# A fused attention and MLP kernel on one core: w_in's first columns sliced by contraction rows, tokens 512 to 767 as two units, later output stores, whole visits

## The chip, the core and the metric

One core of a Trainium2 chip. The time is that of one execution of the program on the device, in microseconds (us); lower is better. The core has a matmul engine (TensorE, PE in the profile; PEld is its loading of weights), a vector engine (VectorE, DVE), a scalar engine (ScalarE, ACT), a general engine (GpSimd, POOL) and an engine that here only issues transfers (SyncE, SP). Each runs its own instruction list in order, and waits for others by semaphores. 16 DMA engines move data between the chip's memory (HBM) and on-chip memory; transfers are issued here by SP and POOL. Matmuls write to PSUM, eight banks of 2 KB in each of 128 partitions.

## The reference

Linear attention with decay, and then a two-layer network, over 4 batches, 8 heads, 768 positions, 64 numbers a head:

```python
for b in range(nb):                      # blocks of 64 positions
    intra = einsum('bhic,bhjc->bhij', qb, kb) * Dmask      # lam ** (i-j), j <= i
    intra = einsum('bhij,bhjd->bhid', intra, vb)
    inter = einsum('bhid,bhde->bhie', qb * lam_pow, kv_state)
    out[:, :, sl] = intra + inter
    kv_state = lam_block * kv_state + einsum('bhsd,bhse->bhde', kb * rev_pow, vb)
...
x = out.transpose(0, 2, 1, 3).reshape(3072, 512)
h = x @ w_in                                               # 512 -> 2048
g = where(h >= 1, h, where(h <= -1, 0, (h + 1) ** 2 / 4))
return g @ w_out                                           # 2048 -> 512
```

All inputs and the output are float32.

## The kernel before

**Attention.** q and k are multiplied by powers of lam that depend on the position alone, so that the decay needs no mask of its own, and are rounded to bf16 in the same step ("cast"). What is left is causal linear attention: scores of a block, a mask, scores times v, and the state (a running sum of k times v) times q.

- The first 512 tokens run as four *units* of 256 tokens and 4 heads (`NU = 4`; functions `e_...`, keys `("...", "e", u)`). A unit loads with two neighbouring tokens to a partition, 512 bytes in a row (`e_load`, L313). PE transposes q and k (`e_t`, L334), ACT or DVE copies the result (`e_tc`, L348), PE computes scores (`e_s`, L381), DVE masks them (`e_m`, L393), PE adds to the state (`e_upd`, L356) and forms state times q (`e_sp`, L399) and scores times v (`e_o`, L414; from unit 2 on a PE drain stands ahead of it), and ACT copies the result to `xT` (`e_x`, L431). In a unit the tokens stand even ones first, so the output tiles of these tokens are stored by halves, every other row (`f_out`, L681).
- Tokens 512 to 767 are chunks 4 and 5, of 128 tokens and all 8 heads, with a code of their own: casts at L465, transposes on PE (`f_t`, L471), scores (`f_s`, L565), output and state (`f_visit` and `f_o`, L583 to L602).
- Chunks 6 to 23 (batches 1 to 3) are cast by POOL (q, k; L468) and ACT (v; L458), transposed by a DMA from on-chip memory to on-chip memory that SP issues (`f_tx`, L483), and then computed by 64x64 matmuls in *visits* (`f_visit2`, L536): scores times v and the second half of state times q of chunk c, and, with them, `f_ahead(c + 1)` (L529): the first half of state times q, the scores, and k times v of chunk c + 2 (L515). For `SPLIT = (9, 11)` the visit leaves `f_ahead` out, which then stands as an operation of its own (`("s", 10)`, `("s", 12)`).

Chunks are loaded with 256 bytes in a row (`f_load`, L438), six buffers deep for each of q, k and v.

**Layers 1 and 2.** Six supertiles of 512 tokens. Layer 1 (`f_l1`, L615) multiplies a slice of w_in with `xT`; a group of 8 matmuls of 256 columns (16 of 128 in supertile 1) fills a PSUM bank of the pool `pp_h` (2 banks) or, for three early groups, of `pp_y` (2 banks). ACT applies a Relu (`f_r`, L629), DVE does the rest of the activation in three steps (`f_g`, L631). Layer 2 (`f_l2`, L650) adds up 16 matmuls in `pp_y`, ACT copies them out (`f_y`, L677) into one of eight output buffers (`OB = 8`), POOL stores them (the last supertile: SP).

**Weights.** Nine slices, loaded by POOL with a conversion to bf16 (`load_w`, L171). The first two are 256 columns of w_in each, all 512 rows of them; the rest have 512 columns, or 512 rows of w_out. Loads of chunk 4 wait for weight slice 7 (`GL`, L732).

**What sets the order.** `add(key, engine, ns, fn, needs, due, ...)` describes every operation with a cost in ns, what it needs and a due time; `run_plan` (L196) works through them as if time passed: on the engine that is free first it takes, of the operations whose needs are met by then, the one due first, and writes the instructions down in that order. On the chip each engine then keeps to this list. Layer 1 and 2 are due one `STEP` apart along `l_seq` (L711), which both kernels share; an attention visit is due 3 us before the layer-1 group that needs it, but is placed as soon as it is ready and nothing is due before. Stores of the first four tiles wait for the visit of chunk 9 + y (L896), later ones only for their tile and the plan's delay.

Of the kernel before, what the change touches and what calls it, by code (L numbers as in the profile page):

```python
# [8 lines left out]
F32 = mybir.dt.float32  # L9
# [14 lines left out]
def kernel(  # L24
# [30 lines left out]
    NU = 4  # L55
# [4 lines left out]
    XT, MG, NQT, NQK, NVS, NUB, RING = 6, 6, 4, 4, 5, 4, 3.5  # L60
# [36 lines left out]
    NE = 4  # L97
    pos_ei = const.tile([128, 2, 2], I32)
    nc.gpsimd.iota(pos_ei, pattern=[[2 * C, 2], [1, 2]], base=-S // 2, channel_multiplier=2)
# [68 lines left out]
    WSL = [(0, 0, 2), (0, 2, 4), (0, 4, 8), (0, 8, 12), (0, 12, 16),  # L168
           (1, 0, 4), (1, 4, 8), (1, 8, 12), (1, 12, 16)]

    def load_w(i):  # L171
        x, lo, hi = WSL[i]
        if x == 0:
            return nc.gpsimd.dma_start(out=w_in_sb[:, :, lo * 128:hi * 128], in_=w_in_r[:, :, lo * 128:hi * 128])
        return nc.gpsimd.dma_start(out=w_out_sb[:, lo:hi, :], in_=w_out_r[:, lo:hi, :])

    def w_of(x, f):
        return [("w", i) for i, (y, lo, hi) in enumerate(WSL) if y == x and lo <= f < hi][0]

# [16 lines left out]
    def run_plan(free):  # L196
# [14 lines left out]
        for x in reversed(topo):  # L211
            d = [u.due - u.ns - x.extra - LAT for u in users[x.key] if not u.dma]
            x.due = min(d + ([x.own] if x.own is not None else []), default=1e9)
            if x.dma or x.key[0] in ("l1", "l2"):
                x.due = x.own
# [92 lines left out]
    def get_ub(c):  # L308
        if c not in ubt:
            ubt[c] = ubp.tile([128, HP, D], BF16, name="ub", tag="ub")  # L310
        return ubt[c]

    def e_load(u, x):  # L313
# [3 lines left out]
        ld_dma["e", u, x] = nc.sync.dma_start(  # L317
            out=t, in_=(q, k, v)[x][0, HR * r:HR * r + HR, s0:s0 + 2 * C, :].rearrange("h (p j) d -> p h (j d)", j=2))
        qkv_ld["e", u, x] = t

    def e_cast(u, x, eng):
        sc, r = divmod(u, 2)
        nm, dct = (("qs", qs), ("ks", ks), ("vs", vs))[x]
        t = qkp.tile([128, 2, HR, D], BF16, name=nm, tag=nm)
# [22 lines left out]

    def e_tc(u, i, eng):  # L348
# [7 lines left out]
    def e_upd(u, a):  # L356
        r, after = u % 2, a == 0 and u > 0
# [13 lines left out]
    def e_st(u, a, eng):  # L371

        if u >= NU:
            dst = get_ub(NU - 1)[:, 2 * (u % 2):2 * (u % 2) + 2, :]
        else:
            t = ubt["e", u, a] = ubp.tile([128, 2, D], BF16, name="ue", tag="ue", bufs=4)
            dst = t
# [21 lines left out]
    def e_sp(u):  # L399
        sc = u // 2  # L400
        po = pot["e", u] = [pp_y.tile([128, MS], F32, name="py", tag="py")[:, 0:256].rearrange("p (h q) -> p h q", h=2)
                            for _ in range(2)]
# [9 lines left out]
        e_upd(u, 1)  # L412

    def e_o(u):  # L414
        sc, po, after = u // 2, pot["e", u], u < NU - 2
# [15 lines left out]
    def e_x(u, a, eng):  # L431
        sc, r = divmod(u, 2)
        off = 2 * C * sc + C * a
        (nc.scalar.copy if eng is nc.scalar else eng.tensor_copy)(
            get_xT(0)[:, 2 * r:2 * r + 2, off:off + C], pot["e", u][a])


    def f_load(c, x, wait):  # L438
# [3 lines left out]
        if wait is not None:  # L442
            tc.add_manual_dep(d.ins, w_dma[wait].ins.name, SYNC)
# [8 lines left out]
    def pair(t, hp):  # L452
        return t[:, 2 * hp:2 * hp + 2, :].rearrange("p a d -> p (a d)")

    def cast(c, x, eng):
        if x == 2:
            t = vs[c] = qkp.tile([128, H, D], BF16, name="vs", tag="vs")
# [6 lines left out]
        if c < NCB:  # L464
            eng.tensor_tensor(t, qkv_ld[c, x], tb, op=AX.mult)  # L465
        else:
            h4 = "p (g i) d -> p g i d"
            eng.tensor_tensor(t.rearrange("p (i g) d -> p g i d", g=2), qkv_ld[c, x].rearrange(h4, g=2),  # L468
                              tb.rearrange(h4, g=2), op=AX.mult)

    def f_t(c):  # L471
        ptt[c] = (pp_o.tile([128, 2, HP, 128], BF16, name="po", tag="po") if c == NU
                  else pp_s.tile([128, 2, HP, 128], BF16, name="ps", tag="ps"))
        for i, x in ((1, ks), (0, qs)):
            for hp in range(HP):
                nc.tensor.transpose(out=ptt[c][:, i, hp, :], in_=pair(x[c], hp), identity=ident)

    def f_tc(c, i):
        dct, nm = ((qT, "qT"), (kT, "kT"))[i]
        t = dct[c] = qtp.tile([128, HP, 128], BF16, name=nm, tag=nm)  # L480
        nc.vector.tensor_copy(t, ptt[c][:, i])
# [83 lines left out]
    def f_s(c):  # L565
        for par in range(2):
            pst[c, par] = pp_s.tile([128, HP, 128], F32, name="ps", tag="ps")
        for hp in range(HP):
            for par in range(2):
                for a in range(2):  # L570
                    nc.tensor.matmul(pst[c, par][HD[a], hp, :], lhsT=kT[c][HD[par], hp, HD[a]],  # L571
                                     rhs=qT[c][HD[par], hp, :], start=True, stop=True, skip_group_check=True)

    def f_m(c, par):
        if par == 0:
            sc_sb[c] = scp.tile([128, 2, HP, 128 if c < NCB else 64], BF16, name="sc" if c < NCB else "sd", tag="sc" if c < NCB else "sd")
        if c < NCB:
            nc.vector.tensor_tensor(sc_sb[c][:, par], pst[c, par], _bc(causal, 1, HP), op=AX.mult)
        else:
            nc.vector.tensor_tensor(sc_sb[c][:, par], pst[c, par], _bc(diag, 1, HP), op=AX.mult)  # L580

    def f_o(c):
# [347 lines left out]
```

## Time and profile before

| | us |
|---|---|
| three runs | 208.47, 209.11, 209.81 |
| their median | 209.11 |
| the profiled execution | 207.5 |
| its span (first to last instruction) | 205.8 |
| first layer-1 matmul starts | 16.2 |
| last layer-2 matmul starts | 202.7 |
| TensorE busy | 196.9 |
| ACT, DVE, POOL busy | 120.4, 140.8, 72.3 |
| share of the 16 DMA engines' time, SP's queue and POOL's | 70.5%, 20.6% |

The clock granted to TensorE is 1.00 in every stretch. The profile lists each instruction with its line, its engine, the tile that it writes, start and length, and, where its engine stood idle before it, what ended that idle time ("<-"). Its chain of waits is the work that ended last, followed back step by step; "issue" in it is time in which nothing that the profile shows was waited for. A DMA's landing is given as the time from its issue.

### The profile page before, as it was taken

The page shows a single profiled execution, that of the slowest core. Times are in us where ns is not written, and L with a number is a line of the kernel's source. Part 1 is how long each engine was busy: PE and PEld are TensorE (multiplying, and loading weights), DVE is VectorE, ACT ScalarE, POOL GpSimd, SP SyncE. Part 2 cuts the span into 40 slices and gives each one's busy share as a digit, 9 for nine tenths or more (in the row PEclk, how much of TensorE's full clock was granted, in tenths as well). Part 3 has the DMA queues.
Part 4 walks back from the last instruction along what each step waited for, and adds up shares of the span by engine and source line. Part 5 has one row for each costly group of instructions (what it writes and reads, how often), then busy time and mean ns, then how long its engine had stood idle before and what let it go on. Part 6 is the DMA issues. An engine that isn't in the chain of part 4 may idle for free.

```text
span 205.8 us, 6360 instructions
## 1 busy us (share of the span) xinstructions
PE 196.9 (96%) x2721; PEld 135.7 (66%) x2753; DVE 140.8 (68%) x251; ACT 120.4 (59%) x225; POOL 72.3 (35%) x95
## 2 busy tenths in 40 slices
PE   7789999999999999999999999999999999999994
PEld 2558875457867867767757777766766766666643
DVE  4694997254885985859985998978876656364510
ACT  4476763327676756675674877486585465463421
POOL 6898000264225363474365255445331011010000
PEclk9999999999999999999999999999999999999999
DMA  5999999999999999999999999999942011011112
GB/s 163 301 235 196 198 206 212 219 220 183 132 183 247 138 201 208 258 195 243 193 183 292 173 218 253 194 180 275 204 109 74 3 43 62 0 51 54 51 51 102
DMA packets 94909, 34.48 MB, mean 168 GB/s; under 512 B 82210, under 2 KB 93218, under 8 KB 94882
## 3 DMA queue, kind: packets, MB, share of 16 engines
q1 hardware_dynamic: 88464, 24.65, 70.5%
q0 software_dynamic: 6416, 9.44, 20.6%
q8 instruction: 21, 0.34, 0.7%
q14 instruction: 6, 0.05, 0.1%
q10 hardware_dynamic: 2, 0.00, 0.0%
HBM read 27.26 MB, written 6.29 MB: 163 GB/s over the span
## 4 chain that ended last, share of the span: by engine, by line
PE 91%; SPq 3%; DMA 3%; issue 2%; DVE 0%; ACT 0%
PE ph L621 41%; PE py L654 38%; SPq L317 3%; DMA x1f<-in_k_dram 3%; PE py L664 2%; PE ps L515 1%; PE py L621 1%; PE ps L507 1%; PE pu L542 1%; PE po L542 1%; PE po L526 1%; PE py L423 1%; PE pu L526 0%; DVE ks L330 0%; PE ps L571 0%
## 5 line engine op out<-in xcount | busy, mean ns | idle before, releaser
L621 PE MATMUL ph<-xT,w_in_sb 128*128 128x256 bf16 (+1 forms) x872 | 94.0, 257 | 0.0
L629 ACT ACTIVATE r<-ph,one 128x512 bf16<-128x512 f32 x93 | 63.8, 687 | 45.2 <-PE ph L621 38.7
L621 PEld LDWEIGHTS <-w_in_sb 128*128 128x128 bf16 x896 | 76.3, 98 | 19.6 <-issue 0.2
L654 PE MATMUL py<-w_out_sb,gT 128*128 128x512 bf16 x338 | 86.0, 379 | 2.3 <-issue 1.1
L654 PEld LDWEIGHTS <-gT 128*128 128x128 bf16 x368 | 34.9, 98 | 28.4
L637 DVE TENSOR_SCALAR t<-r 128x1024 bf16<-128x1024 bf16 x48 | 22.5, 468 | 32.8 <-ACT r L629 32.4
L645 DVE TENSOR_TENSOR gT<-w,t 128x1024 bf16<-128x1024 bf16 x48 | 39.0, 812 | 1.4
L640 DVE TENSOR_TENSOR w<-r,t 128x1024 bf16<-128x1024 bf16 x48 | 38.8, 808 | 1.6
L468 POOL TENSOR_TENSOR kq<-x1f,tkd 128x512 bf16<-128x512 f32 x18 | 20.4, 1131 | 33.2 <-DMA x1f<-in_k_dram 23.4
L468 POOL TENSOR_TENSOR kq<-x0f,tqd 128x512 bf16<-128x512 f32 x18 | 19.7, 1093 | 23.8 <-DMA x0f<-in_q_dram 23.7
L688 POOL DMA_DIRECT2D out_dram<-osb x16 | 9.2, 573 | 32.6 <-ACT osb L679 32.6
L679 ACT COPY osb<-py 128x512 f32<-128x512 f32 x23 | 13.5, 585 | 11.3 <-PE py L654 6.9
L580 DVE TENSOR_TENSOR sd<-ps,diag 128x256 bf16<-128x256 f32 x36 | 13.5, 417 | 3.7 <-PE ps L515 3.5
L458 ACT CAST vs<-x2f 128x512 bf16<-128x512 f32 x20 | 12.4, 618 | 4.9 <-DMA x2f<-in_v_dram 4.5
L554 DVE TENSOR_TENSOR st<-st,ps 128x256 f32<-128x256 f32 x30 | 12.5, 415 | 0.5
L559 ACT CAST us<-st 128x512 bf16<-128x512 f32 (+1 forms) x18 | 10.4, 579 | 1.3 <-DVE st L554 1.2
L465 POOL TENSOR_TENSOR kq<-x0f,tqd 128x512 bf16<-128x512 f32 x2 | 2.4, 1178 | 20.8 <-DMA x0f<-in_q_dram 20.8
L563 ACT CAST xT<-po 128x256 bf16<-128x256 f32 x18 | 6.8, 377 | 4.5 <-PE pu L526 4.0
L563 ACT CAST xT<-pu 128x256 bf16<-128x256 f32 x18 | 6.7, 374 | 2.3 <-PE po L526 2.3
L542 PEld LDWEIGHTS <-vs 64*64 64x64 bf16 x288 | 3.7, 107 | 6.5 <-issue 5.9
L396 DVE TENSOR_TENSOR sc<-ps,mask 128x512 bf16<-128x512 f32 x8 | 5.2, 682 | 2.1 <-PE ps L388 2.1
L515 PE MATMUL ps<-vs,kq 64*64 64x64 bf16 x264 | 6.2, 196 | 0.0
(96 smaller groups left out, 134.3 us busy)
## 6 DMA issues: line engine op xcount, KB each, us to landing
x0f<-in_q_dram SPq DMA_DIRECT2D x24, 256.0 KB, 5.6
x1f<-in_k_dram SPq DMA_DIRECT2D x24, 256.0 KB, 4.8
x2f<-in_v_dram SPq DMA_DIRECT2D x24, 256.0 KB, 5.4
out_dram<-osb POOLq DMA_DIRECT2D x16, 256.0 KB, 4.0
w_out_sb<-in_moe_w_out_dram POOLq DMA_DIRECT2D x4, 512.0 KB, 14.4
w_in_sb<-in_moe_w_in_dram POOLq DMA_DIRECT2D x3, 512.0 KB, 7.8
out_dram<-osb POOLq DMA_DIRECT2D x8, 128.0 KB, 4.6
out_dram<-osb SPq DMA_DIRECT2D x3, 256.0 KB, 2.0
```

The costliest lines, as they stand in the source:

```text
L458: (nc.scalar.copy if eng is nc.scalar else eng.tensor_copy)(t, qkv_ld[c, x])
L468: eng.tensor_tensor(t.rearrange("p (i g) d -> p g i d", g=2), qkv_ld[c, x].rearrange(h4, g=2), tb.rearrange(h4, g=2), op=AX.mult)
L554: nc.vector.tensor_tensor(st[c][:, a], st[c][:, 0] if a else st[c - 1][:, 1], kv[c][a], op=AX.add)
L563: nc.scalar.copy(out=get_xT(s)[:, :, off:off + 64], in_=po_of(c, a))
L580: nc.vector.tensor_tensor(sc_sb[c][:, par], pst[c, par], _bc(diag, 1, HP), op=AX.mult)
L621: nc.tensor.matmul(ph[:, j * m:(j + 1) * m], lhsT=w_in_sb[:, ko, (ni + j) * 128:(ni + j + 1) * 128], rhs=xT[s][:, ko, part * m:(part + 1) ...
L629: nc.scalar.activation(out=r_t[grp][:, i, :], in_=ph_t[s, ni, part], func=AF.Relu, bias=one[:, 0:1])
L637: nc.vector.tensor_scalar(t_t[grp], r, 0.5, 1.0, op0=AX.mult, op1=AX.min)
L640: nc.vector.tensor_tensor(w_t[grp], r, t_t[grp], op=AX.subtract)
L645: nc.vector.tensor_tensor(gT[s][:, f - RW * n:f, part * m:(part + 1) * m], w_t[grp].rearrange("p a (b m) -> p (a b) m", m=m), t_t[grp].rea ...
L654: nc.tensor.matmul(py_t[s, ms], lhsT=gT[s][:, ko, ms * 128:(ms + 1) * 128], rhs=w_out_sb[:, ko, :], start=(ko == 0), stop=(ko == FO - 1))
L679: nc.scalar.copy(out=osb[s, ms], in_=py_t[s, ms])
```

## The change

It has four parts.

1. The first 512 columns of w_in are loaded as two slices of 256 rows by 512 columns, in place of two of 512 rows by 256 columns. The first two groups of layer 1 become three operations: `l1k`, with the first 256 rows for both groups (8 matmuls), and then the other rows for the one and the other (4 each).
2. Tokens 512 to 767 become units 4 and 5 (`NU = 6`, of which `NS = 4` are the start), with loads of 512 bytes in a row, `e_t2` that transposes k and q in one go, and scores and state in one operation. Their results use banks of `pp_h` (unit 4), `pp_o` and `pp_u` (unit 5). The code of chunks 4 and 5 goes.
3. `e_x` writes `xT` in the tokens' natural order (with a step of two elements), so that every tile is stored by one DMA. Every store by POOL now waits for the visit of chunk y + 11 (or the last) and for the store before it.
4. `SPLIT = ()`: all visits have their `f_ahead`.

The core of the diff (what only renames is left out):

```diff
-    NU = 4
+    NS, NU = 4, 6
...
-    WSL = [(0, 0, 2), (0, 2, 4), (0, 4, 8), (0, 8, 12), (0, 12, 16),
+    KS = [slice(0, 2), slice(2, 4)]
+    WSL = [(0, 0, 4, 0), (0, 0, 4, 1), (0, 4, 8), (0, 8, 12), (0, 12, 16),
            (1, 0, 4), (1, 4, 8), (1, 8, 12), (1, 12, 16)]
...
+            return nc.gpsimd.dma_start(out=w_in_sb[:, ks, lo * 128:hi * 128], in_=w_in_r[:, ks, lo * 128:hi * 128])
...
+    def e_t2(u):
+        t = pp_o.tile([128, 2, 2, 2, 128], BF16, name="po", tag="po")
+        for i in (1, 0):
+            ptt["e", u, i] = t[:, i]
+            for j in range(2):
+                for hp in range(2):
+                    nc.tensor.transpose(out=t[:, i, j, hp, :],
...
     def e_sp(u):
         sc = u // 2
+        if u < NS:
+            po = [pp_y.tile([128, MS], F32, name="py", tag="py") for _ in range(2)]
+        elif u == NS:
+            po = [pp_h.tile([128, MS], F32, name="ph", tag="ph") for _ in range(2)]
+        else:
+            po = [pp_o.tile([128, MS], F32, name="po", tag="po"), pp_u.tile([128, MS], F32, name="pu", tag="pu")]
...
-        e_upd(u, 1)
+        if u < NS:
+            e_upd(u, 1)
...
     def e_x(u, a, eng):
...
-            get_xT(0)[:, 2 * r:2 * r + 2, off:off + C], pot["e", u][a])
+            get_xT(sc // 2)[:, 2 * r:2 * r + 2, off:off + C].rearrange("p h (q j) -> p h j q", j=2),
+            pot["e", u][a].rearrange("p h (j q) -> p h j q", j=2))
...
+    def f_l1k(ks, nis):
+        for ni in nis:
+            if ks.start == 0:
+                ph_t[0, ni, 0] = pp_h.tile([128, MS], F32, name="ph", tag="ph")
+            for j in range(2):
+                for ko in range(ks.start, ks.stop):
+                    nc.tensor.matmul(ph_t[0, ni, 0][:, j * 256:(j + 1) * 256],
+                                     lhsT=w_in_sb[:, ko, (ni + j) * 128:(ni + j + 1) * 128],
+                                     rhs=xT[0][:, ko, 0:256],
+                                     start=(ko == 0 and j == 0), stop=(ko == KO - 1), skip_group_check=True)
...
     def f_out(s, ms):
-        if s == 0:
-            for j in range(2):
-                nc.gpsimd.dma_start(out=out[m0:m0 + 128, :].rearrange("(p j) n -> j p n", j=2)[j], in_=osb[s, ms][HD[j], :])
-        elif s < NST - 1:
+        if s < NST - 1:
             nc.gpsimd.dma_start(out=out[m0:m0 + 128, :], in_=osb[s, ms])
...
-    SPLIT = (9, 11)
+    SPLIT = ()
...
+    for u in range(NS, NU):
+        od = l_due[1, 1, 0, 0] - LEAD - (3000 if u == NS else 0)
+        for x, e in ((1, KE[u - NS]), (0, "POOL"), (2, "ACT")):
+            add(("cast", "e", u, x), e, 540 if x == 2 else {"DVE": 605, "POOL": 1040}[e],
...
+        add(("t", "e", u), "PE", mm(*[128] * 8), lambda u=u: e_t2(u),
+            [("cast", "e", u, 0), ("cast", "e", u, 1), ("qT", "e", u - 1), ("kT", "e", u - 1)], due=od - 6000, extra=FILL)
...
+        add(("s", "e", u), "PE", 400, lambda u=u: (e_s(u), e_upd(u, 0)),
...
+        add(("o", "e", u), "PE", 700 + (130 if u == NU - 1 else 0), lambda u=u: (e_sp(u), e_o(u), f_kv(NU, get_sk()) if u == NU - 1 else None),
...
-            add(("st", y), "POOL" if s < NST - 1 else "SP", 1600 if s == 0 else 800 if s < NST - 1 else 550, lambda a=(s, ms): f_out(*a),
-                [("y", y), ("o", 9 + y)] if s == 0 else [("y", y), ("st", y - 1) if y > CPS else None],
+            add(("st", y), "POOL" if s < NST - 1 else "SP", 800 if s < NST - 1 else 550, lambda a=(s, ms): f_out(*a),
+                [("y", y), ("st", y - 1) if y else None, ("o", min(y + OGATE, NCH - 1)) if s < NST - 1 else None],
```

`OGATE` is 11, `KE` and `TE` put both units' casts of k and copies of the transposes on DVE. The unit's `e_o` keeps its drain (`u < NS - 2` alone is without).

## The prediction

> **What bounds the kernel now.** I read the page first (busy shares, slices, chain), then the chain by windows, then the built program's order on each engine for both kernels, then the engines' timelines and single DMA issues.
>
> The page, parts 1, 2 and 4; a digit is the busy share of a slice of 5.1 us:
>
> ```profile
> span 205.8 us, 6360 instructions
> ...
> PE 196.9 (96%) x2721; PEld 135.7 (66%) x2753; DVE 140.8 (68%) x251; ACT 120.4 (59%) x225; POOL 72.3 (35%) x95
> ...
> DMA  5999999999999999999999999999942011011112
> ...
> PE 91%; SPq 3%; DMA 3%; issue 2%; DVE 0%; ACT 0%
> ```
>
> TensorE (PE) is on the chain for 91% of the span, and from 16.2 us, where the first layer-1 matmul starts, the chain is hardly anything else. So time comes from matmul work, from switches between 64x64 attention tiles and full tiles, or from a new wait of PE. The DMA engines are full until about 150 us and idle after: inputs arrive at the pace of the DMA stream.
>
> The chain around two kinds of attention visit (start, us, what):
>
> ```profile
> 71.67 0.89 PE ph L621 x16
> 72.57 0.15 PE pu L542 x2
> ...
> 73.07 0.19 PE ps L515 x16
> 73.26 0.16 issue
> 73.42 0.81 PE py L654 x3
> ...
> 75.98 0.15 PE po L542 x2
> ...
> 76.30 0.54 PE py L654 x2
> 76.83 0.05 issue
> 76.89 1.24 PE py L654 x5
> 78.13 1.75 PE ph L621 x16
> 79.88 0.15 PE po L526 x2
> ...
> 80.19 0.12 PE ps L515 x8
> 80.31 0.98 PE ph L621 x8
> ```
>
> A whole visit (chunk 8) lasts 72.57 to 73.26 = 0.69 us; the split one (chunk 9) is 0.32 at 75.98 and 0.43 at 79.88. The first two matmuls of a visit cost 0.15 where later pairs cost 0.03, and the first layer-1 group behind it 0.98 where others cost 0.87: 0.12 in, 0.11 out.
>
> ACT around the same visits (start, us, what, idle before it):
>
> ```profile
> 71.66 0.62 ACT L458 CAST vs<-x2f 128x512 bf16<-128x512 f32 x1
> 78.42 0.62 ACT L458 CAST vs<-x2f 128x512 bf16<-128x512 f32 x1 [0.91 <-DMA x2f<-in_v_dram]
> ```
>
> These cast v of chunks 10 and 11. Chunk 8's visit computes k.v of chunk 10, so it needs the first: done 72.28, visit at 72.57, 0.3 to spare. PE does not wait in before, but only just.
>
> I call 8 layer-1 matmuls of 256 columns (16 of 128) or 4 of layer 2 a group: 0.87 us (0.895 with 128 columns). Time is told by groups done.
>
> **The change part by part.**
>
> *Row slices of w_in.* The order on PE keeps its places: 8 layer-1 matmuls behind unit 3's scores, 8 more behind its output. Before, the first started at 16.18 as the update matmuls ended (16.07+0.12), and the first slice had landed at 16.1 (issue 10.71, 5.4 to landing); both slices stay 512 KB of f32. A sooner landing would meet a busy PE: 0. The first Relu loses 17.26 and comes at about 18.7, the second at 19.5, because both halves now end in the second eight; their two PSUM banks are asked for again at 20.07 and 20.94: covered. If each slice landed up to 0.2 later PE would wait that long; taken 0 (0 to 0.2). The strided xT copies (L434, 0.37 and 0.42) have until 19.1 and end at 18.7; one half longer would still fit: 0 (0 to 0.2). Tables grow from 32 to 48 columns, far before the load that the chain waits for (k of unit 3, 7.75 to 13.13): 0.
>
> *Tokens 512 to 767 as units, PE's work.* Before, from the first transposes (40.16) to the end of the layer-2 group behind chunk 6's scores (56.04): 15.88 us, of which 7 layer-2 groups x 0.866 and 6 layer-1 groups x 0.895 = 11.43; attention and switches 4.45. After, by the order: transposes 0.45; scores 0.34 (L388 x16) + update 0.12 (L364 x8) + transposes 0.45 + switches 0.23 = 1.14; unit 4's state and output with the drain by unit 3's row (17.22 to 18.21, 0.99, and 0.11 out, less update 0.12), then scores 0.34 and update 0.12 = 1.44; unit 5 the same, with k.v of chunk 6 (L515 0.19), 1.17; chunk 6's scores 0.54. Sum 4.74: **+0.3** (0 to +0.6, if the drains are hidden, or as long again). DVE's masks and POOL's casts keep number and size; ACT trades two 0.58 copies for four of 0.38 and small state copies, in a stretch where it is 40% busy (40 to 50 us).
>
> *Waits in that stretch.* The first transposes now stand two groups earlier, at 38.4. They need POOL's cast of q, which before started at 38.14 when its load landed and took 1.04. Unit loads come faster: in the opening DVE waits for every third one at 10.44 and 13.16, 0.90 us a load, while 256-byte runs of chunks 4 to 6 (POOL, 38.14 and 41.59) come every 1.15. So q lands about 0.4 earlier and PE waits 0.4; 0.85 if not earlier, 0 if 0.85 earlier. On DVE the cast of unit 5's k now stands ahead of unit 4's transposed copies, which the scores need: that k lands at about 39.5 (36.8 + 3 x 0.9), cast and two copies end at 41.1, and PE comes at 41.0 to 41.4. Together **+0.3** (0 to 1.3); the lower half, since one wait eats the other.
>
> At this row a rule can be weighed. The Trainium skill, *DMA: Bandwidth & Descriptors*, Specifications, puts line rate at transfers of 512 B and more, and the HBM limit of a core at about 358 GB/s. By that, an estimate, a unit load of 256 KB would take 0.73 us, not 0.90; the six loads would come another 1.0 us earlier, and the waits here and below would be gone: the third rival. The opening already has 512-byte runs and shows 0.90, so the trace does not agree, and I stay with it.
>
> *No split visits.* Each split costs 0.32 + 0.43 + two ways out (0.10, 0.11) = 0.96; a whole visit 0.69 + 0.11 = 0.80. Twice: **-0.3**.
>
> *Visits come earlier.* With the same sequence of layers, the order puts chunk 6's visit after 41 groups (44 before), 7 after 47 (49), 8 after 51 (56), 9 after 57 together with chunk 10's scores (63 before), 12 to 15 two to four earlier; from 16 on all is equal. PE reaches chunk 8's visit at 72.57 - 5 x 0.89 + 0.3 + 0.3 = 68.7. It needs v of chunk 10, landed at 71.64 before (issue 65.67, 6.0 to landing). The stream gains 6 x 0.26 = 1.6 from the unit loads, and about 1.2 from the store issued at 63.10 that now comes much later (from v of chunk 9 to v of 10 took 7.0 us with a store between, the step before it 5.8 without). Landing 68.8, cast until 69.5: a wait of 0.8. A second store (issued 70.17) goes too, and overlapped the last 1.5 us; half of that: **+0.4** (0 to 3.7; 3.7 if nothing comes earlier). What is queued behind that wait is layer 1 and 2, so all of it counts. Chunk 9's visit then comes at 75.3 and its v (78.39 - 1.6 - 2.2, cast 0.7) is ready at 75.3. Later ones gain another store each and have more room.
>
> *Later stores.* POOL issues one store of 256 KB for two of 128 KB in the first four tiles: four issues of 0.55 less, POOL is 35% busy: 0. Eight output buffers must hold until tile 8's copy. The tightest in the order is tile 9's copy (104.2 before), which waits for tile 1's store behind POOL's cast of k of chunk 16 (106.35 before). Seven tiles' stores of some 1.1 us and the 1.6 go ahead of it: about 97, store at 98.4, landing 4 to 6.7 later: 102.4 to 105.1. ACT waits up to 0.9; the Relus behind it have two PSUM banks, one is asked for 1.7 us after the other: 0 (0 to 2). The stores held until the last visit (about 178) land 2 us each before SP's last three (191 on), and the last store's path is the same.
>
> **The sum**: 0 + 0.3 + 0.3 - 0.3 + 0.4 + 0 = +0.7 us. The profiled execution took 207.5 us (span 205.8, 1.7 around it): 208.2. The median shown is 209.11, 1.6 above it: **209.8 us**.
>
> **The rivals.**
> - *The stream is no earlier* (slower). Place: v of chunk 10 at L458, before chunk 8's visit. For it: DMA is full, and the visits move 3 to 6 groups. Against: six loads and two stores are plainly lighter or later. Price 3.7 there and 0.6 at chunk 9, against my 0.4: 209.8 + 3.9 = 213.7. It decides from a landing of 70.2 on (wait 2.1).
> - *ACT waits for a store* at tile 9, longer than two banks cover. For: releases now hang on visits 11 chunks on. Against: the sum above. Some 2 us: 211.8 at most, 210.5 in its middle.
> - *Everything is hidden*: both waits gone, +0.3 - 0.3: 209.1. For it: the second store may count in full, another 0.5 us, and unit 5's k may land sooner than at the opening's pace, which was set with SP issuing every 0.5 to 1.1 us. Against: DMA is full. The rule above speaks for it too.
> - *It does more than it says* (faster by 2.1 and more): an earlier start of layer 1. PE is busy up to 16.18, and no row shows such a sum: 207.0 and less.
>
> **How the numbers follow.** Forecast with its waits 0.50, hidden 0.25, stream late 0.12, store wait 0.08, earlier start 0.05. A measurement of this kernel can tell about 1% from no change. Slower by over 1% is above 211.2: 0.12, half of the store wait 0.04, and 0.02 of the forecast's upper end: 0.18. Faster 0.05, within 0.77. The range goes from the hidden case with the runs' scatter (209.1 - 0.9) to where the store wait ends: 208.2 to 211.8; the late stream (0.12) and the earlier start (0.05) lie outside.
>
> **What would show it.** Right: layer 1 starts at 16.2; PE waits under 0.5 us each near 38 and 41 and 0 to 1 us at chunk 8's visit near 69, ended by ACT's cast of v; no piece of a visit without scores; v of chunk 10 landed near 68.5; no idle time of ACT from a store at tile 9 over 1 us. Wrong: PE gaps of over 2 us between 65 and 80, or unit loads at the old 1.15.

## The result and the profile after

| | before | after |
|---|---|---|
| median of 20 runs each, us | 208.40 | 209.75 |
| lowest and highest | 207.72, 209.81 | 208.75, 211.42 |
| the profiled execution | 207.5 | 210.08 |
| its span | 205.8 | 206.8 |

The ratio is 1.0062, with a 95% interval of 1.0044 to 1.0079: 1.3 us (0.0062 x 208.40) slower. The interval leaves out 1, so the loss is told apart from nothing, though it is smaller than 1%. The profiled run of after has 3.3 us around its span, that of before 1.7; the spans are the better pair, +1.0.

The page of after, parts 1, 2 and 4:

```profile
span 206.8 us, 6441 instructions
...
PE 199.0 (96%) x2777; PEld 135.5 (66%) x2777; DVE 142.6 (69%) x251; ACT 121.3 (59%) x228; POOL 70.7 (34%) x91
...
DMA  5999999999999999999999999994952001011112
...
PE 91%; SPq 3%; DMA 3%; DVE 1%; issue 1%; ACT 0%
```

At this scale nothing has changed: PE has the same share of span and chain, and DMA is full until about 150 us. In the last line DVE has 1% of the chain where it had 0% (and "issue" 1% where it had 2%). DVE's share is where to look. The chain of before at the start of layer 1 (start, us, what):

```profile
16.19 1.04 PE ph L621 x8
...
17.80 0.42 PE py L423 x16
18.21 0.98 PE ph L621 x8
19.19 0.87 PE py L621 x8
```

The same stretch of after:

```profile
16.38 1.00 PE ph L582 x8
...
17.40 0.44 ACT xT L445
17.85 0.14 ACT ue L384
...
18.56 0.42 PE py L434 x16
18.98 0.56 PE ph L582 x4
...
19.56 0.45 DVE xT L445
...
20.06 0.50 PE ph L582 x3
20.56 0.87 PE py L571 x8
```

The sixteen layer-1 matmuls around unit 3's output ran without a wait before. Now copies into xT stand between them, and the first group on py starts at 20.56 instead of 19.19: 0.19 of it because layer 1 starts later, 1.18 inside this stretch. The waits of after, 15 to 21 us (engine line waited for: us in total, times, longest us):

```profile
DVE xT L445 <- PE ph L582: 2.1, 1, 2.1
ACT xT L445 <- PE ph L582: 1.9, 2, 1.1
...
PE ph L582 <- DVE xT L445: 0.4, 1, 0.4
```

and of before:

```profile
DVE xT L434 <- PE py L423: 0.9, 1, 0.9
...
ACT xT L434 <- PE py L423: 0.4, 1, 0.4
```

In after the copies of units 2 and 3 wait for layer-1 matmuls, and then a layer-1 matmul waits for a copy. There is no reason for either in the data: these copies write tokens 256 to 511 of xT, and these matmuls read tokens 0 to 255. In before the copies waited for nothing but the matmuls whose result they carry. The loss has two halves. ACT's copy of the state (ue, 17.85) is queued behind the waiting copy into xT, and PE waits 0.43 for it, until 18.03; then a layer-1 matmul waits another 0.43 for DVE's copy, until 20.06. Scores times v of unit 3 start 2.24 after the first layer-1 matmul instead of 1.62 (18.56 - 16.32, and 17.80 - 16.18), 0.62 of the loss; the other 0.61 comes after that.

Where the later losses of the forecast were to be, there are none. PE of after around the first transposes and scores of units 4 and 5 (start, us, instruction; an idle time would stand at the end of the row):

```profile
39.87 0.39 PE L353 MATMUL po<-ident,qs 128*128 128x128 bf16 x4
...
41.91 0.42 PE L393 MATMUL ps<-qT,kT 64*64 64x128 bf16 x16
```

and ACT's cast of v of chunk 10, which is done (68.60 + 0.61 = 69.21) before PE comes to chunk 8's visit at 69.46:

```profile
68.60 0.61 ACT L465 CAST vs<-x2f 128x512 bf16<-128x512 f32 x1
```

For comparing stages between runs that start layer 1 at different times, I use two numbers from each profile: from the first layer-1 matmul to the first layer-1 matmul on py, by PE's timeline (before 19.03 - 16.18 = 2.85; after 20.40 - 16.32 = 4.08), and from the first layer-1 matmul to the end of the last layer-2 group, from these last rows of the chain of before and of after:

```profile
199.46 3.51 PE py L664 x32
```

```profile
200.44 3.51 PE py L625 x32
```

which gives 202.97 - 16.18 = 186.79 before and 203.95 - 16.32 = 187.63 after, **+0.84**. So 1.23 is lost in the first 4 us of layer 1, and 0.39 is won back behind it.

### The profile page after: what moved, and what is told of

The parts are those of the page before. It is cut to its first block, busy times and chain, and to the rows that moved or that the text cites. A ratio compares the mean times of both kernels' runs of the same rounds, so it can differ in the third digit from the quotient of the medians.

```text
span 206.8 us, 6441 instructions
## 1 busy us (share of the span) xinstructions
PE 199.0 (96%) x2777; PEld 135.5 (66%) x2777; DVE 142.6 (69%) x251; ACT 121.3 (59%) x228; POOL 70.7 (34%) x91
## 4 chain that ended last, share of the span: by engine, by line
PE 91%; SPq 3%; DMA 3%; DVE 1%; issue 1%; ACT 0%
PE ph L571 40%; PE py L615 39%; SPq L314 3%; DMA x1f<-in_k_dram 3%; PE py L625 2%; PE ps L507 1%; PE py L571 1%; PE ps L499 1%; PE po L534 1%; PE pu L534 1%; PE ph L582 1%; PE po L518 1%; PE py L434 1%; PE ps L393 0%; PE po L353 0%
## 5 line engine op out<-in xcount | busy, mean ns | idle before, releaser
L571 PE MATMUL ph<-xT,w_in_sb 128*128 128x256 bf16 (+1 forms) x856 | 92.6, 257 | 0.0
L615 PE MATMUL py<-w_out_sb,gT 128*128 128x512 bf16 x368 | 92.0, 379 | 0.0
L571 PEld LDWEIGHTS <-w_in_sb 128*128 128x128 bf16 x880 | 75.0, 98 | 19.9
L606 DVE TENSOR_TENSOR gT<-w,t 128x1024 bf16<-128x1024 bf16 x48 | 40.5, 844 | 1.5
L472 POOL TENSOR_TENSOR kq<-x0f,tqd 128x512 bf16<-128x512 f32 x18 | 20.7, 1152 | 25.4 <-DMA x0f<-in_q_dram 25.3
L645 POOL DMA_DIRECT2D out_dram<-osb x20 | 11.1, 559 | 37.1 <-ACT osb L640 37.1
L329 POOL TENSOR_TENSOR qs<-x0f,tqe 128x512 bf16<-128x512 f32 x6 | 6.3, 1046 | 20.5 <-DMA x0f<-in_q_dram 19.9
L465 ACT CAST vs<-x2f 128x512 bf16<-128x512 f32 x18 | 11.0, 613 | 0.5 <-DMA x2f<-in_v_dram 0.5
L401 DVE TENSOR_TENSOR sc<-ps,mask 128x512 bf16<-128x512 f32 x12 | 7.8, 682 | 4.9 <-PE ps L393 4.9
L329 DVE TENSOR_TENSOR ks<-x1f,tke 128x512 bf16<-128x512 f32 x6 | 5.2, 868 | 2.8 <-DMA x1f<-in_k_dram 2.8
```

Of the source, the lines that this page charges most:

```text
L329: eng.tensor_tensor(t, src, _bc(tab_e[x][:, 2 * sc:2 * sc + 2, HR * r:HR * r + HR], 3, D), op=AX.mult)
L571: nc.tensor.matmul(ph[:, j * m:(j + 1) * m], lhsT=w_in_sb[:, ko, (ni + j) * 128:(ni + j + 1) * 128], rhs=xT[s][:, ko, part * m:(part + 1) ...
L606: nc.vector.tensor_tensor(gT[s][:, f - RW * n:f, part * m:(part + 1) * m], w_t[grp].rearrange("p a (b m) -> p (a b) m", m=m), t_t[grp].rea ...
L615: nc.tensor.matmul(py_t[s, ms], lhsT=gT[s][:, ko, ms * 128:(ms + 1) * 128], rhs=w_out_sb[:, ko, :], start=(ko == 0), stop=(ko == FO - 1))
```

## The experiments

Theory **T1**: the write with a step of two elements makes the program take the copies to tokens 256 to 511 and the reads of tokens 0 to 255 for the same data, and sets semaphores between them. Rivals: the row slices of w_in make the wait (**T1b**), or the strided copies are merely slower (**T1c**). Later **T2** was added: once that wait is gone, PE meets the loads of units 4 and 5, or the last slices of w_out, and waits there instead. Its rivals are in the expectations. All runs, with the ratio to runs of the kernel before on the same chip; each median of an experiment is of 6 to 12 runs. "To py" and "layers" are the two numbers from the profiled run, a single one of each kernel, the second against before:

| run | median, us | ratio (95%) | to py | layers |
|---|---|---|---|---|
| after | 209.75 | 1.0062 (1.0044 to 1.0079) | 4.08 | +0.84 |
| e1_plain_copies | 209.39 | 1.0034 (1.0005 to 1.0064) | 2.86 | +2.35 |
| e2_two_tiles | 209.63 | 1.0049 (1.0029 to 1.0068) | 2.85 | +0.81 |
| e3_column_slices | 209.10 | 1.0030 (1.0007 to 1.0052) | 3.95 | +0.99 |
| e4_before_strided | 209.39 | 1.0048 (1.0022 to 1.0073) | 3.95 | +1.37 |
| e7_one_group_later | 208.87 | 1.0027 (1.0005 to 1.0048) | 2.91 | +1.01 |
| e3b_columns_two_tiles | 208.79 | 1.0030 (1.0014 to 1.0046) | 2.85 | -0.34 |
| e5_split | 209.65 | 1.0078 (1.0050 to 1.0107) | 4.92 | +1.85 |
| e6_early_stores | 209.47 | 1.0056 (1.0034 to 1.0079) | 4.08 | +0.80 |
| e8_read_in_order | 209.22 | 1.0057 (1.0030 to 1.0084) | 4.02 | +0.73 |
| e8_plain_dest | 209.31 | 1.0049 (1.0025 to 1.0074) | 2.85 | +2.31 |
| e9_plain_dest_later | 208.84 | 1.0029 (1.0008 to 1.0050) | 2.85 | -0.34 |
| e10_loads_earlier | 208.99 | 1.0048 (1.0028 to 1.0067) | 2.85 | +0.98 |

The medians of the kernel before beside them are 208.38 (e1 to e4), 208.24 (the next four) and 208.25 (the last four). A ratio's interval is about 0.25% to each side, 0.5 us, so "to py" decides on the early wait, and the medians decide little below half a microsecond.

### The strided write, taken away and put in alone

e1_plain_copies: whole runs written again, the first tiles stored by halves for it.

```diff
-            get_xT(sc // 2)[:, 2 * r:2 * r + 2, off:off + C].rearrange("p h (q j) -> p h j q", j=2),
-            pot["e", u][a].rearrange("p h (j q) -> p h j q", j=2))
+            get_xT(sc // 2)[:, 2 * r:2 * r + 2, off:off + C], pot["e", u][a])
...
-        if s < NST - 1:
+        if m0 < S:
+            for j in range(2):
+                nc.gpsimd.dma_start(out=out[m0:m0 + 128, :].rearrange("(p j) n -> j p n", j=2)[j], in_=osb[s, ms][HD[j], :])
+        elif s < NST - 1:
```

> The changed kernel with one part undone: the copies of the first four units into xT write whole runs of 128 columns again, as in the kernel before, and the tiles of tokens below 768 are stored by halves for it. Row slices, six units, later stores and no split visits stay. Theory T1 (the two-element step in the write makes the copies of tokens 256 to 511 and the layer-1 reads of tokens 0 to 255 wait for each other, though they touch other columns): no copy into xT waits for a layer-1 matmul any more, the first py group of layer 1 starts at 19.2 to 19.4 instead of 20.56, and the median is 1.1 to 1.4 below the changed kernel; up to 0.7 of that may be given back where PE, now at 38.4, waits for the cast of q before the transposes of units 4 and 5 or for v of chunk 10. Rival T1b (the row slices cause it): py still starts after 20.3 and the time is within 0.3 of the changed kernel. Rival T1c (the strided copies are only slower each, 0.45 against 0.38): py starts 0.1 to 0.2 earlier and the gain is no more than 0.2.

e2_two_tiles: the strided write kept, tokens 0 to 255 and 256 to 511 in tiles of their own.

```diff
...
+    def get_x0(p):
+        if p not in x0:
+            x0[p] = xp.tile([128, KO, MS // 2], BF16, name="xTh", tag="xTh", bufs=2)
+        return x0[p]
...
-            get_xT(sc // 2)[:, 2 * r:2 * r + 2, off:off + C].rearrange("p h (q j) -> p h j q", j=2),
+            (get_x0(sc)[:, 2 * r:2 * r + 2, C * a:C * a + C] if sc < 2 else get_xT(sc // 2)[:, 2 * r:2 * r + 2, off:off + C])
+            .rearrange("p h (q j) -> p h j q", j=2),
...
-                                 rhs=xT[s][:, ko, part * m:(part + 1) * m],
+                                 rhs=xT[s][:, ko, part * m:(part + 1) * m] if s else x0[part][:, ko, :],
...
-                                     rhs=xT[0][:, ko, 0:256],
+                                     rhs=x0[0][:, ko, :],
```

> The changed kernel, its strided copies kept, but the x of tokens 0 to 255 and that of tokens 256 to 511 lie in two tiles of their own; for room the later x tiles rotate over two buffers instead of three. Theory T1 (a false overlap between strided writes to tokens 256 to 511 and reads of tokens 0 to 255 in one tile): no copy waits for layer 1, the first py group starts at 19.2 to 19.5, the median falls by 1.0 to 1.4 from the changed kernel, up to 0.7 of it given back at the transposes of units 4 and 5 (near 38.4) and at chunk 8's visit. Rival T1b (row slices): py still after 20.3, within 0.3 of the changed kernel. Rival T1c (slower copies): no gain here, since the copies are as slow as before.

e3_column_slices: the slices by columns again, the strided write kept (the planner's time for these two slices, 1350 ns in after, goes back to the 1800 of before).

```diff
-    WSL = [(0, 0, 4, 0), (0, 0, 4, 1), (0, 4, 8), (0, 8, 12), (0, 12, 16),
+    WSL = [(0, 0, 2), (0, 2, 4), (0, 4, 8), (0, 8, 12), (0, 12, 16),
...
-        if n1 == 0:
+        if False:
...
-        add(("l1", n1), "PE", mm(*[256] * 4) if n1 < 2 else mm(*[MS // n] * (KO * n)),
-            (lambda i=i: f_l1k(KS[1], (i,))) if n1 < 2 else lambda a=(s, i, n, p, on_y[n1]): f_l1(*a),
+        add(("l1", n1), "PE", mm(*[MS // n] * (KO * n)),
+            lambda a=(s, i, n, p, on_y[n1]): f_l1(*a),
...
```

> The changed kernel with its main part undone: the first two slices of w_in are columns 0 to 255 and 256 to 511 over all rows again, and layer 1 of the first groups runs whole. Six units, strided copies, single stores, later stores and no split visits stay. Theory T1 (strided copies and reads of one tile): the copies still wait for layer 1 and the first py group starts at 20.0 to 20.8; within 0.4 of the changed kernel. Rival T1b (the row slices cause the loss): no copy waits for layer 1, py starts at 19.2 to 19.4, and the time is 1.0 to 1.4 below the changed kernel.

e4_before_strided: the kernel before, with the strided write alone (and its first tiles stored in one piece, as the order of the tokens then wants).

```diff
-            get_xT(0)[:, 2 * r:2 * r + 2, off:off + C], pot["e", u][a])
+            get_xT(0)[:, 2 * r:2 * r + 2, off:off + C].rearrange("p h (q j) -> p h j q", j=2),
+            pot["e", u][a].rearrange("p h (j q) -> p h j q", j=2))
...
-        if s == 0:
-
-            for j in range(2):
-                nc.gpsimd.dma_start(out=out[m0:m0 + 128, :].rearrange("(p j) n -> j p n", j=2)[j], in_=osb[s, ms][HD[j], :])
-        elif s < NST - 1:
+        if s < NST - 1:
```

> The kernel before with one part of the change alone: its four units' copies into xT write with a step of two elements, and its first tiles are stored in one piece each. Theory T1: the copies of units 2 and 3 wait for the layer-1 matmuls that run at 16.2 to 17.2 and on, the first py group starts at 20.2 to 20.8 instead of 19.19, and the time is 1.0 to 1.4 above the kernel before. Rival T1b (row slices): no such wait, py at 19.2 to 19.3, within 0.2 of the kernel before. Rival T1c (copies 0.07 slower each): py 0.1 to 0.2 later, at most 0.2 above the kernel before.

By "to py" the four runs agree with T1 and not with its two rivals. Without the step in the write, or with two tiles, the stretch has its old length (2.86 and 2.85). With the step it is 3.95, with column slices just as in the kernel before, so the row slices are not needed for it (T1b falls). The waits of e4_before_strided, 15 to 21 us:

```profile
DVE xT L434 <- PE ph L622: 2.2, 1, 2.2
ACT xT L434 <- PE ph L622: 2.1, 2, 1.2
```

These are the waits of after, in a kernel that has nothing else of the change but the stores in one piece. It is 1.10 longer up to py and 1.37 to the end, and 1.0 us slower by the ratio. T1c has a true core: the copy takes ACT 448 ns on average with the step in its write (two tiles) and 375 without; but two tiles keep that cost and lose the wait.

The times tell something else. e1 and e2 were expected to win 1.0 to 1.4, less up to 0.7 given back later, and their medians are 0.4 and 0.1 below after. PE of e2_two_tiles where units 4 and 5 begin:

```profile
39.42 0.40 PE L360 MATMUL po<-ident,qs 128*128 128x128 bf16 x4 [0.57 <-POOL qs L336]
...
41.90 0.42 PE L400 MATMUL ps<-qT,kT 64*64 64x128 bf16 x16 [0.20 <-DVE qT L367]
```

PE comes to the transposes 1.2 earlier than in after (38.47 against 39.64), and waits for POOL's cast of q and then for DVE's copies behind the cast of unit 5's k. Measured from the first layer-1 matmul, the scores start at 41.90 - 16.37 = 25.53 here and at 41.91 - 16.32 = 25.59 in after: all that the start gained is gone. Part of this is not the earlier PE, though: k of unit 5, behind whose cast the copies stand, landed at 40.47 here and at 39.62 in after. The profiled run of e1 loses more, and its loads came later still (k of unit 5 at 42.1).

### The units one group later, with rows and with columns

e7_one_group_later: e2_two_tiles, and the planner is told that a row slice takes longer.

```diff
-            due=i * 1e-3, dma=2650 if len(WSL[i]) == 3 else 1350)
+            due=i * 1e-3, dma=2650 if len(WSL[i]) == 3 else 1800)
```

> The kernel with two x tiles (strided copies kept, no false overlap), and the planner is told that a row slice takes 1800 instead of 1350 ns: this moves the transposes, scores and outputs of units 4 and 5 one group (0.87) later in PE's order and the visits of chunks 8 and 9 one and two groups later; nothing else. Theory T2 (with the early wait gone, PE runs into the loads of units 4 and 5 instead: 0.57 for the cast of q and 0.64 for the copies behind the cast of unit 5's k): the first of these waits is gone and the second is at most 0.2; against that, up to 0.3 is lost where layer 1 of the next tile starts on x of unit 5, one group closer; the median is 0.6 to 1.1 below the two-tile kernel, near 208.7 and within 0.5 of the kernel before. Rival T2b (the loss lies behind 58 us, in visits or stores, and only looks like a wait at 40): less than 0.3 below the two-tile kernel.

e3b_columns_two_tiles: the edits of e2_two_tiles and e3_column_slices together. e3_column_slices itself has this later order too, since the planner counts its slices at 1800, so its median below that of after is not the columns' doing alone.

> The same as the kernel one group later, but the first two slices of w_in are columns again and layer 1 of the first groups runs whole: the two differ in the row slices alone, PE's order from the 25th group on is the same. The prediction on record gives the row slices 0 (0 to +0.2): medians of the two within 0.3 of each other. Rival (halving the rows costs, since no Relu can start before the second half): columns are 0.4 or more faster. Rival (rows help, an earlier start): columns are 0.4 or more slower.

The two medians are 0.08 apart: rows or columns make no difference that these runs can tell. From e2_two_tiles to e7_one_group_later the ratio falls from 1.0049 to 1.0027, 0.46 us, less than the 0.6 to 1.1 expected but the way that T2 says; the two intervals overlap, so this is a hint and no proof. The profiled run of e3b_columns_two_tiles shows the layers without a wait of PE over 0.16: -0.34 against before. The one of e7_one_group_later shows how little room the start has: its transposes wait for nothing any more, but before them layer 2 waited 1.08 for a slice of w_out, at 30.88. So PE came to the transposes later by that wait as well as by the planned 0.87, and the run does not show that one group is enough.

### Splits and stores put back

e5_split:

```diff
-    SPLIT = ()
+    SPLIT = (9, 11)
```

> The changed kernel with the visits of chunks 9 and 11 split again. The prediction on record has the two splits at 0.16 each: 0.3 slower than the changed kernel, with four visit pieces more and PE's time of 64x64 entries 0.12 and exits 0.11 once more per split. Rival (the split takes pressure off v of chunk 11): 0.3 or more faster.

The medians (209.65, and 209.75 for after in other runs) do not tell 0.3. In the profiled runs, from the first py group to the end, e5_split gives back 4.92 - 2.85 - 1.85 = 0.22 and after 4.08 - 2.85 - 0.84 = 0.39: two splits cost 0.17 there, half of what was expected. Its start is not to be compared: the clock granted to PE was 0.63 from 8 to 22 us in that run.

e6_early_stores:

```diff
-                [("y", y), ("st", y - 1) if y else None, ("o", min(y + OGATE, NCH - 1)) if s < NST - 1 else None],
+                [("y", y), ("o", 9 + y)] if s == 0 else [("y", y), ("st", y - 1) if y > CPS else None],
```

> The changed kernel with the output stores released as before: the first four tiles with the visits of chunks 9 to 12, the others at once. The prediction on record gives later stores 0 by themselves, but counts 1.2 us of earlier landing for v of chunk 10 to them: v of chunk 10 then lands at 68 to 69 instead of 67.06, its cast ends after PE comes to chunk 8's visit at 69.5 by at most 0.6, and the time is 0 to 0.6 above the changed kernel. Rival (holding the stores costs: they collide with the end, or output buffers run out): the time is 0.3 or more below it.

v of chunk 10 landed at 66.70, no later than in after (67.06), and the layers took about the same (+0.80). The stores' place is worth nothing that these runs can tell. It is not what brought v forward either: here that store is issued at 64.75 and the load of v at 62.19, ahead of it, while in before a store (63.10) went ahead of that load (65.67).

### What makes the wait: the view, not the step

e8_read_in_order:

```diff
-            get_xT(sc // 2)[:, 2 * r:2 * r + 2, off:off + C].rearrange("p h (q j) -> p h j q", j=2),
-            pot["e", u][a].rearrange("p h (j q) -> p h j q", j=2))
+            get_xT(sc // 2)[:, 2 * r:2 * r + 2, off:off + C].rearrange("p h (q j) -> p h q j", j=2),
+            pot["e", u][a].rearrange("p h (j q) -> p h q j", j=2))
```

> The changed kernel, but the copies of the units into xT go through the tokens in their order: the step of two elements is in the read of PSUM, and what is written is whole runs of 128 columns; both sides are still given as views of four dimensions. Theory T1 in its narrow form (the wait is a semaphore that the program sets because a write given in four dimensions is taken to cover all that lies between its ends): the copies still wait for layer 1 and the first py group starts 1.2 to 1.4 later, measured from the first layer-1 matmul, than the 2.85 of the kernel before. Rival T1d (the step in memory is what counts): no wait, 2.8 to 2.9 from the first layer-1 matmul to the first py group.

e8_plain_dest:

```diff
-            get_xT(sc // 2)[:, 2 * r:2 * r + 2, off:off + C].rearrange("p h (q j) -> p h j q", j=2),
-            pot["e", u][a].rearrange("p h (j q) -> p h j q", j=2))
+            get_xT(sc // 2)[:, 2 * r:2 * r + 2, off:off + C],
+            pot["e", u][a].rearrange("p h (j q) -> p h q j", j=2))
```

> The same copies as with the read in order, the built instruction has the same shapes, but the destination is given plainly, as in the kernel before. Narrow T1: no copy waits for layer 1 and the first py group comes 2.8 to 2.9 after the first layer-1 matmul; then theory T2 holds (the loads of units 4 and 5 end the gain near 39 and 42): the median is 0 to 0.5 below the changed kernel, as for the two tiles. Rival T1d: the wait is the same in both kernels with this copy.

In both kernels the copy goes through its destination in order, in whole runs, and reads PSUM through the same view. The waits of e8_read_in_order, 15 to 21 us:

```profile
DVE xT L445 <- PE ph L582: 1.9, 1, 1.9
ACT xT L445 <- PE ph L582: 1.8, 2, 1.1
```

and of e8_plain_dest:

```profile
DVE xT L445 <- PE py L434: 0.8, 1, 0.8
ACT xT L445 <- PE py L434: 0.6, 2, 0.4
```

The copies are the same, 374 and 375 ns on ACT; only the way in which their destination is written down differs, and with it the wait (to py 4.02 and 2.85). So the wait is a dependency that the program sets for a destination given as this rearranged view of four dimensions, and no conflict in memory. That it covers all between the view's ends is not shown, but fits what waits for what: xT holds four rows of 512 tokens in each partition, a copy to tokens 256 to 511 of two rows encloses tokens 0 to 255 of the second one. The runs show only that reads and writes through the plain view are told apart and those through the rearranged one are not.

Again the time hardly moves. PE of e8_plain_dest later on, and ACT at that place:

```profile
42.57 1.02 PE L615 MATMUL py<-w_out_sb,gT 128*128 128x512 bf16 x4 [0.86 <-ACT osb L640]
```

```profile
41.41 0.62 ACT L327 CAST vs<-x2f 128x512 bf16<-128x512 f32 x1 [1.49 <-DMA x2f<-in_v_dram]
```

ACT stood idle until v of unit 4 landed; the copy that frees the bank of layer 2 is queued behind that cast, and PE waited for it. Before that, PE had waited 1.13 for a slice of w_out. Both are the start's stream of loads, which came late in this profile: k of unit 4 landed at 38.43, against 36.89 in e8_read_in_order.

### The remedy with later units, and earlier loads

e9_plain_dest_later is e8_plain_dest with the edit of e7_one_group_later.

> The plain destination, and units 4 and 5 one group later in PE's order. T2: both early losses are gone; from the first layer-1 matmul to the end of the last layer-2 group the time is 0.3 below the kernel before in a run whose loads are not late (the columns with two tiles showed 0.34), and the median is 0.6 to 1.1 below the changed kernel, 208.5 to 208.9, still at or up to 0.6 above the kernel before. Rival T2b: within 0.3 of the kernel with the plain destination alone.

e10_loads_earlier is e8_plain_dest with the loads of units 4 and 5 released by the second slice of w_out instead of the third (these are the two slices that the expectation means):

```diff
-    GL = {(NS, 1): 7}
+    GL = {(NS, 1): 6}
```

> The plain destination with the units in their old place in PE's order, but the loads of units 4 and 5 are released by the third of the four w_out slices before the last, not by the one before the last, so they are issued some 2.2 us earlier and run beside the last two slices. T2 in the form that the stream of all bytes is the limit: the waits at the transposes shrink, the last w_out slices land 1 to 2 later and layer 2 waits for them; within 0.4 of the plain destination. Rival T2c (only the order of the loads is the limit): both waits near 39 and 42 vanish, layer 2 does not wait, and the time is 0.6 to 1.0 below the plain destination.

e9 has the layers at -0.34, as expected. Its last rows end like this, with layer 1 started at 18.01:

```profile
200.95 3.51 PE py L625 x32
```

But in this profile layer 1 started 1.5 later than in e8_plain_dest (16.51), and k of unit 4 landed only 0.2 later (38.59 against 38.43). So PE found the loads ready by the late start as much as by the later place in its order, as it did in e3b_columns_two_tiles (17.91); -0.34 is what the layers take without waits, not what the later order wins. Its ratio is 1.0029, 0.7 us below after (the intervals just overlap), and still 0.6 above before. e10 does as T2 says: the same ratio as e8_plain_dest (1.0048 and 1.0049), with PE waiting for the last slice of w_out, and still for the cast. That slice landed at 37.92, 0.4 later than in e8_plain_dest, where 1 to 2 were expected:

```profile
37.97 1.89 PE L615 MATMUL py<-w_out_sb,gT 128*128 128x512 bf16 x7 [0.60 <-DMA w_out_sb<-in_moe_w_out_dram]
...
40.53 0.40 PE L353 MATMUL po<-ident,qs 128*128 128x128 bf16 x4 [0.45 <-POOL qs L329]
```

No version beat the kernel before.

## Why the forecast was right in its number and wrong in its reasons

The number, 209.8 against 209.75, is right by luck: two errors cancel. It starts from 209.11, the median of three runs; over 20 runs the kernel before has 208.40, 0.7 less. And the sum of +0.7 stands against +1.3. By its terms:

- *Row slices, 0.* Right as far as these runs can tell: 208.87 with rows and 208.79 with columns in the same order.
- *Strided copies, 0 (0 to 0.2).* **This is the step that failed**: "have until 19.1 and end at 18.7; one half longer would still fit". The allowance of one half covers their length (448 ns against 375), and the slack was read rightly. What was not asked is which new waits the changed view brings: a copy that waits for layer 1, and layer 1 and the state's copy that wait for it. They cost 1.23 in the profiled run, and the kernel before with this write and the stores in one piece is 1.0 slower: five times the bound.
- *Units' work on PE, +0.3.* By the same count as in the forecast, after has 57.41 - 39.80 = 17.61 us with 9 layer-2 and 6 layer-1 groups: 17.61 - 9 x 0.866 - 6 x 0.895 = 4.45, what it was before. The term is 0; that the switches and drains priced singly were partly hidden is the likely reason, and not shown.
- *Waits at the transposes and scores, +0.3 (0 to 1.3).* 0 in after, since PE came 1.4 late. The place was right: without the early wait PE does wait there. In after the loads landed as forecast (q of unit 4 at 37.69, k of unit 5 at 39.62). By them, without the early wait, the cast of q (done at 38.89) and then the copies behind the cast of unit 5's k (done at 41.04) would have held PE some 0.4, an estimate close to the forecast. In the run of e2_two_tiles it was 1.2, with k of unit 4 landing 0.5 later and k of unit 5 0.85 later.
- *No split visits, -0.3.* -0.17 by one profile each of e5_split and after. All of the layers without waits are at -0.34 (e3b, e9), where the forecast had +0.3 - 0.3 = 0; the other 0.17 is not assigned.
- *Chunk 8's visit, +0.4.* 0: v of chunk 10 landed at 67.06 instead of 68.8, its cast ended at 69.21, and PE came at 69.46. The load was issued 2.9 earlier than in before (62.73 against 65.67) and took 4.3 instead of 6.0: the stream gained more than was counted, and e6_early_stores shows that this was not the stores' doing. What did it was not tried.
- *Later stores, 0.* Right as far as six runs of e6_early_stores can tell.

The rule weighed in the forecast came out as the trace had it before: the unit loads of after landed at 36.85, 37.69, 38.60, 39.62 and 40.48, 0.91 apart. The Trainium skill (*DMA: Bandwidth & Descriptors*, Specifications) would give 0.73 as an estimate; the trace does not agree, and the rival that leaned on it lost this reason. Its two waits were indeed gone in after, but because PE came late.

None of the rivals was what happened. That a copy could wait for layer 1 was not among them, though the forecast listed waits of PE on loads at three places. And losses at the start need not add up: a PE that is held early finds the loads ready later. That fits why four kernels without the early wait (e1, e2, e8_plain_dest, e10) are by their ratios only 0.3 to 0.6 us faster than after. It need not be all of it: by the estimate above only some 0.4 of the 1.2 would go that way with the loads of after's profile, and the profiles of these four had later loads.

**What stays open.** With all of these waits gone (e9, e3b), the layers are 0.34 shorter than before, but the medians are 0.5 to 0.6 longer. Their profiled runs started layer 1 at 18.01 and 17.91, before at 16.19; after at 16.38 shows that the six units do not force that. What was late in these two is PE itself, here in after and then in e9_plain_dest_later:

```profile
6.45 0.40 PE L343 MATMUL po<-ident,ks 128*128 128x128 bf16 x4
```

```profile
6.91 0.63 PE L343 MATMUL po<-ident,ks 128*128 128x128 bf16 x4
```

The same four transposes of unit 0 take half as long again, and so do the others of e9 and e3b up to 16.1, though the granted clock reads 1.00 there; their chains up to layer 1 hold no load, where those of before and after wait for k of unit 3.

The openings differ in one more thing. POOL's first cast of q takes 1.50 to 1.58 in seven of the twelve profiles of six-unit kernels (e1, e3, e7, e3b, e8_plain_dest, e9, e10), where DVE's cast of k beside it takes 0.69; it takes 1.04 in the other five and in the two profiles of kernels with four units (before, e4), where DVE's takes 1.2 to 1.6. The seven start layer 1 at 16.5 to 18.0 and get k of unit 4 at 37.6 to 39.1; the other five start at 16.2 to 16.4 (e5_split, with its low clock, at 18.0) and get it at 36.9 to 38.0. So "layers" compares two profiles fairly only where they opened alike. Whether the six-unit kernels open slowly more often than before, which could explain the medians, can't be settled with one profile of each.

## What to carry to other kernels

When an edit changes how a tile is indexed, list every instruction that touches the tile and ask which new waits the dependencies may set; here a rearranged view of a part was taken for more than that part. Where it can be done, give the destination plainly and put the permutation into the read, then look in the waits view for an engine that waits for a matmul whose result it does not use. And before counting the removal of a wait as a gain, find the next thing that this engine needs: here what the loads feed was ready less than 1 us before PE, held early, came for it. And before a stage is compared between two profiles, look whether they opened alike.

## What the runs showed of the hardware

- A copy of 128x256 from PSUM by ACT takes 448 ns (e2_two_tiles) when it writes bf16 with a step of two elements and 375 in whole runs (before); the same step in the f32 read of PSUM costs nothing (374 in e8_read_in_order). On DVE it is 445 against 424, one copy in each run.
- The time around the span is 1.7 us in all 99 runs of before and e4_before_strided. It was over 2.0, up to 3.3, in 16 of the 132 runs of the kernels with six units. What they have in common besides the units, and why, was not tried.
- The granted clock was not always 1.00 in the opening: 0.63 from 8 to 22 us in the profiled run of e5_split, while it was 1.00 there in before and in after. In the runs of e3_column_slices and e4_before_strided it was 0.5 to 0.6 from 8 to 12 us. In those of e9_plain_dest_later and e3b_columns_two_tiles it reads 1.00, and four transposes still took 0.61 to 0.63 us, against 0.40 in after, up to 16 us.
